# Eight instead of 55 extra pieces in the products of zeros at the head of a fused attention and feed-forward kernel

## The chip, the cores and the metric

The kernel runs on one core of a Trainium2 chip. The metric is the device time of one execution in microseconds, lower is better. Engines: TensorE (PE, with weight loads PEld and products), VectorE (DVE), ScalarE (ACT), GpSimd (POOL), SyncE (SP, which here issues DMAs only).

## The reference

Two parts, one after the other. The first is an attention in which keys and values are mixed block by block by a matrix P (8x8 for each batch and head) that five rounds of exponential and normalisation make from sort_net:

```python
# q, k, v: (4, 8, 768, 64); sort_net: (4, 8, 8, 8); block = 96
P = sort_net
for _ in range(5):
    P = np.exp(P - P.max(-1, keepdims=True))
    P = P / (P.sum(-1, keepdims=True) + 1e-09)
    P = P / (P.sum(-2, keepdims=True) + 1e-09)
k_sorted = einsum('bhij,bhjcd->bhicd', P, k_b)      # v_sorted likewise
scores = (q_b @ k_sb^T) / 8                         # inside a block of 96
attn = softmax(scores)
x = (attn @ v_sb) -> (3072, 512)
```

The second is a feed-forward over the 3072 rows: `h = x @ w_in` (512 to 2048), `g = h * cos(h)`, `out = g @ w_out` (2048 to 512).

## The kernel before

The rows of x are made in eight groups n = 0 to 7 of 384 rows (half a batch each), with four blocks u of 96 in a group. A table written out by hand, PLAN, sets the order in which every engine gets its work: a line such as `S 2 0 B` calls the function S with its arguments, and each engine works through its own instructions in that order. The calls that matter here:

- `v0`, `vb`, `vg`: products that mix the blocks of v (into `vS`); `vp`, `vp2` copy v into another order on POOL (`vperm`, L992), which some of these products read.
- `S` / `T`: scores; `M`, `X`: row maximum and difference on DVE; `E`: exponential on ACT into one of three buffers `p_buf`; `TP` / `TE` or `TD`: the transpose of p, by PE in the first groups and by a transposing DMA on SP's queue (L1396) in the later ones; `AV` (L1423): attention times values, whose weights are the transposed p; `N`: its normalisation on DVE; `XP` / `XE` or `XD` (L1445): the transpose into `xT`, by PE or by a transposing DMA.
- `U` (L1487): x times w_in; `C`: the sine on ACT; `G`: the product on DVE; `D` (L1532): g times w_out; `O`, `W`: out to memory.

Before the table runs, the head of the kernel issues the loads of q, k and v (POOL's queue, in that order, then w_in), and the five rounds on P run on ACT and DVE. Meanwhile PE multiplies zeros: `warm` is a 128x128 tile of zeros, and `keep_warm(times, t, cols)` (L1052) issues `times` products of `cols` columns into a tile that nothing reads. As long as `pieces` (L1050, set from MORE) lasts, a product is cut into up to four pieces of the same total of columns, each piece with a weight load and a product of its own. The head has, in this order: 15 (L1062, ahead of the first transposes of q, `q_twice`, L1135), 2 (L1157), and 6, 2 and 4 through `idle` (L1143). Later single calls in the first part of the plan (in `kp`, `v0`, `TP`, `AV`) come after `pieces` has run out.

With 55, all 15 opening products are cut in four (45 extra pieces), then the 2 (6 extra), then one of the first `idle` in four and one in two.

Of the kernel before, what the change touches and what calls it, by code (L numbers as in the profile page):

```python
# [13 lines left out]
ALU = mybir.AluOpType  # L14
AX = mybir.AxisListType

MORE = 55
PLAN = """\
vp 32
kp 0 B 1  # L20
# [811 lines left out]
def kernel(  # L832
# [16 lines left out]
    B, H, S, D = q.shape  # L849
# [129 lines left out]
    vv = kv[:, :128 * D].rearrange("p (c d) -> p d c", d=D)  # L979
    VQ = 16  # L980

    def v_permute(rows, lo=0, halves=True):

        for z in range(lo, D, VQ):
            dst = vperm[rows, :CD].rearrange("p (d c) -> p d c", d=D)[:, z:z + VQ]
            src = vv[rows, z:z + VQ, :blk]
            if halves:
                dst = dst.rearrange("p d (x t) -> p d x t", x=2)  # L990
                src = src.rearrange("p d (t x) -> p d x t", x=2)
            nc.gpsimd.tensor_copy(dst, src)  # L992
# [56 lines left out]

    pieces = [MORE]  # L1050

# [526 lines left out]
    def vp(lo):  # L1578
        v_permute(slice(0, 64), lo, False)

    def vp2(lo, hi):
        v_permute(slice(lo, hi))

    def z_vperm():
        nc.gpsimd.memset(vperm[:64, :D // 2 * blk], 0.0)

# [13 lines left out]
    def spv():  # L1600
# [4 lines left out]
        vb=vb, vbe=vbe, vg=vg, vge=vge, S=S, M=M, X=X, E=E, TD=TD, TP=TP, TE=TE, AV=AV, N=N,  # L1605
        XD=XD, XP=XP, XE=XE, QP=QP, QE=QE, QD=QD, U=U, C=C, G=G, U4=U4, C4=C4, G4=G4, D=D4,
        O=O, W=W, Lq=load_q, Lw=load_w_out, Lk=Lk, Lv=Lv, Lpk=Lpk, Lpv=Lpv, hk=hk, hp=hp_, hq=hq,
        vp=vp, vp2=vp2, z_vperm=z_vperm, p_pads=p_pads, pk2=pk2, bl2=bl2, sp2=sp2, spv=spv,
        ones=ones, z_turned=z_turned, zeros=zeros_between)
    words = {"A": (A,), "V": (V,), "B": (big, "big"), "c": (acc, "acc"), "-": (None,)}  # L1610
    for line in PLAN.split("\n"):
# [47 lines left out]
```

## Time and profile before

| | |
|---|---|
| median of 3 runs | 236.39 us (236.24 to 236.46) |
| profiled execution | 237.13 us, of which the span from first to last instruction is 235.3 us |
| PE busy, products | 96% of the span, 2270 recorded |
| PE weight loads | 62%, 2293 |
| DVE, ACT, POOL busy | 73%, 64%, 40% |
| granted clock of PE, mean | 0.998 |
| read from and written to memory | 27.27 MB and 6.29 MB |

The profile is one execution. A line such as `1.00 5.78 PE L1058 ...` gives start and duration in us, engine, line of the kernel, operation, what is written and read, shapes and count; in brackets is how long the engine stood idle before it and what ended that. Queues of DMAs have a line each with packets, MB and the time of these packets as a share of 16 DMA engines; "q8 instruction" is the queue on which instructions are fetched.

### The profile page before, as it was taken

The page shows a single profiled execution, that of the slowest core. Times are in us where ns is not written, and L with a number is a line of the kernel's source. Part 1 is how long each engine was busy: PE and PEld are TensorE (multiplying, and loading weights), DVE is VectorE, ACT ScalarE, POOL GpSimd, SP SyncE. Part 2 cuts the span into 40 slices and gives each one's busy share as a digit, 9 for nine tenths or more (in the row PEclk, how much of TensorE's full clock was granted, in tenths as well). Part 3 has the DMA queues.
Part 4 walks back from the last instruction along what each step waited for, and adds up shares of the span by engine and source line. Part 5 has one row for each costly group of instructions (what it writes and reads, how often), then busy time and mean ns, then how long its engine had stood idle before and what let it go on. Part 6 is the DMA issues. An engine that isn't in the chain of part 4 may idle for free.

```text
span 235.3 us, 5542 instructions
## 1 busy us (share of the span) xinstructions
PE 226.5 (96%) x2270; PEld 146.0 (62%) x2293; DVE 172.3 (73%) x287; ACT 151.3 (64%) x201; POOL 93.8 (40%) x117
## 2 busy tenths in 40 slices
PE   8889999999999999999999999999999999999994
PEld 8567799667656666645666556654565556456553
DVE  5657986787798786896678976899588868555510
ACT  3365976578969858884888746756567456636531
POOL 7669998795980094981709000720000000000000
PEclk9999999999999999999999999999999999999999
DMA  5999999796799779997999539995942570341012
GB/s 75 225 192 205 205 210 231 121 219 174 110 105 178 152 137 147 135 204 160 148 162 84 80 75 133 219 73 103 168 161 51 100 170 0 63 131 45 0 47 89
DMA packets 67257, 31.11 MB, mean 132 GB/s; under 512 B 55968, under 2 KB 62752, under 8 KB 66976
## 3 DMA queue, kind: packets, MB, share of 16 engines
q0 software_dynamic: 24048, 13.64, 44.0%
q1 hardware_dynamic: 42896, 16.92, 35.2%
q8 instruction: 18, 0.29, 0.5%
q10 hardware_dynamic: 288, 0.20, 0.3%
q14 instruction: 7, 0.06, 0.1%
HBM read 27.27 MB, written 6.29 MB: 143 GB/s over the span
## 4 chain that ended last, share of the span: by engine, by line
PE 82%; DMA 7%; ACT 3%; POOL 3%; DVE 2%; issue 2%; POOLq 0%
PE o L1532 32%; PE h L1487 29%; DMA kv<-in_v_dram 5%; PE h L1510 5%; PE av L1423 3%; PE sc L1319 3%; POOL vperm L992 2%; PE ks L1200 2%; PE xps L1457 2%; PE o L1623 2%; PE pps L1405 1%; DMA kv<-p_buf 1%; PE vs L1256 1%; PE vs L1291 1%; ACT c L1493 1%
## 5 line engine op out<-in xcount | busy, mean ns | idle before, releaser
L1532 PE MATMUL o<-w_out_t,gg 128*128 128x512 bf16 x348 | 84.7, 379 | 1.2 <-issue 0.2
L1487 PE MATMUL h<-xT,w_in_t 128*128 128x384 bf16 x448 | 78.2, 326 | 0.4 <-DVE gg L1499 0.2
L1499 DVE TENSOR_TENSOR gg<-c,h 128x768 bf16<-128x768 f32 x56 | 53.0, 949 | 22.4 <-ACT c L1493 22.3
L1493 ACT ACTIVATE c<-h,half_pi 128x768 f32<-128x768 f32 x56 | 50.5, 901 | 25.5 <-PE h L1487 23.3
L1487 PEld LDWEIGHTS <-w_in_t 128*128 128x128 bf16 x448 | 42.4, 98 | 27.5 <-issue 0.9
L1532 PEld LDWEIGHTS <-gg 128*128 128x128 bf16 x368 | 33.3, 98 | 33.0
L1360 DVE TENSOR_REDUCE mx<-sc 96x8 f32<-96x768 f32 (+1 forms) x41 | 31.5, 771 | 3.1 <-PE sc L1319 1.5
L1378 ACT ACTIVATE p_buf<-s 96x768 bf16<-96x768 f32 x32 | 26.3, 841 | 10.1 <-DVE s L1374 7.7
L992 POOL COPY vperm<-kv 64x1536 bf16<-64x1536 bf16 (+1 forms) x10 | 28.1, 2860 | 2.1 <-DMA kv<-in_v_dram 2.1
L1374 DVE TENSOR_TENSOR s<-sc,mx 96x384 f32<-96x384 f32 (+1 forms) x33 | 24.2, 734 | 1.6
L1435 DVE TENSOR_TENSOR xn<-av,r 96x512 bf16<-96x512 f32 x32 | 22.0, 687 | 1.1
L942 POOL DMA_DIRECT2D kv<-in_q_dram x24 | 16.0, 687 | 0.8 <-issue 0.5
L1069 ACT CAST kTs<-ks 128x512 bf16<-128x512 f32 (+1 forms) x18 | 11.0, 633 | 4.8 <-PE ks L1200 4.8
L942 POOL DMA_DIRECT2D q_mem<-in_q_dram x16 | 10.7, 695 | 3.4 <-DMA kv<-in_v_dram 3.1
L1058 PE MATMUL idle<-warm 128*128 128x128 bf16 (+2 forms) x83 | 9.5, 288 | 2.2 <-ACT q_turned L1141 1.2
L1433 DVE RECIPROCAL r<-av 96x8 f32<-96x8 f32 x32 | 6.3, 198 | 6.6 <-PE av L1423 6.6
L1071 DVE COPY kv<-o 128x512 f32<-128x512 f32 (+1 forms) x6 | 3.7, 624 | 10.0 <-PE o L1623 6.8
L1510 PE MATMUL h<-xT,w_in_t 128*128 128x192 bf16 x128 | 11.1, 246 | 0.0
L1319 PE MATMUL sc<-kTs,q_turned 128*128 128x96 bf16 x160 | 11.1, 206 | 0.0
L1058 PEld LDWEIGHTS <-warm 128*128 128x128 bf16 x101 | 8.9, 121 | 3.4 <-issue 1.3
L1319 PEld LDWEIGHTS <-q_turned 128*128 128x128 bf16 x160 | 9.1, 98 | 2.7 <-DVE s L1374 0.2
L1555 POOL CAST held<-q_turned 96x1 f32<-96x1 bf16 x2 | 0.4, 184 | 26.2 <-DMA q_turned<-q_mem 19.3
(119 smaller groups left out, 272.6 us busy)
## 6 DMA issues: line engine op xcount, KB each, us to landing
out_dram<-kv SPq DMA_DIRECT2D x12, 256.0 KB, 2.9
out_dram<-o_s SPq DMA_DIRECT2D x10, 256.0 KB, 3.0
w_in_t<-in_moe_w_in_dram POOLq DMA_DIRECT2D x4, 512.0 KB, 12.4
w_out_t<-in_moe_w_out_dram POOLq DMA_DIRECT2D x4, 512.0 KB, 11.6
kv<-in_k_dram POOLq DMA_DIRECT2D x2, 768.0 KB, 9.5
kv<-in_v_dram POOLq DMA_DIRECT2D x2, 768.0 KB, 13.3
pair<-in_k_dram POOLq DMA_DIRECT2D x2, 768.0 KB, 10.2
kv<-in_v_dram POOLq DMA_DIRECT2D x6, 256.0 KB, 5.7
```

What stands on the lines that cost most here:

```text
L942: nc.gpsimd.dma_start(out=q_heads[:, i, :, e], in_=src[:, ih * IC + i, :, e])
L992: nc.gpsimd.tensor_copy(dst, src)
L1319: nc.tensor.matmul(out, q_of(n, hp)[:, x:x + 128], keys_of(n, u, h2, hp), start=True, stop=True)
L1360: nc.vector.reduce_max(mx[:], s_view(n, u, hp), axis=AX.XY if n < 2 else AX.X)
L1374: nc.vector.tensor_tensor(s, sc, mx.to_broadcast(list(s.shape)), op=ALU.subtract)
L1378: nc.scalar.activation(p[:, :, :blk], s_t.pop((n, u)).rearrange("p e h c -> p (e h) c"), AF.Exp, scale=scale)
L1435: nc.vector.tensor_tensor(xn.rearrange("p h e d -> p e h d"), avv[:, :, :, :D], r.to_broadcast([blk, 2, H2, D]), op=ALU.mult)
L1487: nc.tensor.matmul(o[:, f2, x * w:(x + 1) * w], w_in_t[:, kk, f * 128:(f + 1) * 128], xT[n][:, kk, x * w:(x + 1) * w], start=(kk == 0), st ...
L1493: nc.scalar.activation(c[:], ps["h", n, fp][:, :, :TC], AF.Sin, bias=half_pi[:, 0:1])
L1499: nc.vector.tensor_tensor(gt[n, fp // 2][:, f:f + 2], ps.pop(("c", n, fp))[:], ps.pop(("h", n, fp))[:, :, :TC], op=ALU.mult)
L1510: nc.tensor.matmul(o[:, part, f2 * w:(f2 + 1) * w], w_in_t[:, kk, f * 128:(f + 1) * 128], xT[0][:, kk, h * w:(h + 1) * w], start=(kk == 0) ...
L1532: nc.tensor.matmul(out_ps[n, ts][:], gt[n, q][:, f % 4, ts * 128:(ts + 1) * 128], w_out_t[:, f, :], start=(f == 0), stop=(f == FC - 1))
```

## The change

`MORE` is 8 instead of 55. The first two opening products are cut in four and the third in three; all that follow are whole, of 512 columns. The columns of each call are the same, and 47 weight loads and 47 products are fewer. The code that builds the program also gets a function `vq` and an upper end for `v_permute`, which the plan does not call.

```diff
-MORE = 55
+MORE = 8
...
-    def v_permute(rows, lo=0, halves=True):
+    def v_permute(rows, lo=0, halves=True, hi=D):
...
-        for z in range(lo, D, VQ):
+        for z in range(lo, hi, VQ):
...
+    def vq(lo, hi, z):
+        v_permute(slice(lo, hi), z * VQ, True, (z + 1) * VQ)
```

On PE, at the end of the cut part of the opening products; before, the last pieces ahead of the transposes of q (`qps` from `q_mem`):

```order
L1058 MATMUL idle<-warm 128x128
L1058 LDWEIGHTS warm
L1058 MATMUL idle<-warm 128x128
L1135 LDWEIGHTS q_mem
L1135 MATMUL qps<-ident,q_mem 64x4x24
```

and now, where the cut products pass into whole ones:

```order
L1058 MATMUL idle<-warm 128x128
L1058 LDWEIGHTS warm
L1058 MATMUL idle<-warm 128x170
L1058 LDWEIGHTS warm
L1058 MATMUL idle<-warm 128x171
L1058 LDWEIGHTS warm
L1058 MATMUL idle<-warm 128x171
L1058 LDWEIGHTS warm
L1058 MATMUL idle<-warm 128x512
L1058 LDWEIGHTS warm
```

The first transpose of q is PE's row 121 of 4588 before, and row 47 of 4494 now.

On PE, in the first `idle` (six products between two lots of transposes of q), before:

```order
L1058 MATMUL idle<-warm 128x128
L1058 LDWEIGHTS warm
L1058 MATMUL idle<-warm 128x256
L1058 LDWEIGHTS warm
L1058 MATMUL idle<-warm 128x256
L1058 LDWEIGHTS warm
L1058 MATMUL idle<-warm 128x512
```

and now, up to the transposes behind them, all of them whole:

```order
L1058 MATMUL idle<-warm 128x512
L1058 LDWEIGHTS warm
L1058 MATMUL idle<-warm 128x512
L1135 LDWEIGHTS q_mem
L1135 MATMUL qps<-ident,q_mem 64x4x24
```

From here on PE's rows are the same, each 94 earlier in its stream of instructions: the first product of `bl` (L1180) is row 297 before and row 203 now. The rows of DVE, ACT, POOL and SP are as many as before (250, 149, 65 and 54) and in the same order.

More of the change, by code (lines that the diff above doesn't have):

```diff
@@ L1607 @@
         O=O, W=W, Lq=load_q, Lw=load_w_out, Lk=Lk, Lv=Lv, Lpk=Lpk, Lpv=Lpv, hk=hk, hp=hp_, hq=hq,
-        vp=vp, vp2=vp2, z_vperm=z_vperm, p_pads=p_pads, pk2=pk2, bl2=bl2, sp2=sp2, spv=spv,
+        vp=vp, vp2=vp2, vq=vq, z_vperm=z_vperm, p_pads=p_pads, pk2=pk2, bl2=bl2, sp2=sp2, spv=spv,
         ones=ones, z_turned=z_turned, zeros=zeros_between)
```

## Prediction

> **What bounds the kernel.** I read the page first, then the chain of waits, the start of the timeline, the DMA queues in narrow stretches, and the stretches around the transposing DMAs.
>
> ```profile
> PE 226.5 (96%) x2270; PEld 146.0 (62%) x2293; DVE 172.3 (73%) x287; ACT 151.3 (64%) x201; POOL 93.8 (40%) x117
> q8 instruction: 18, 0.29, 0.5%
> PE 82%; DMA 7%; ACT 3%; POOL 3%; DVE 2%; issue 2%; POOLq 0%
> ...
> 2.72 12.68 DMA kv<-in_v_dram
> 15.46 5.57 POOL vperm L992 x2
> 21.81 0.94 PE vs L1256 x16
> ```
>
> TensorE (PE) is busy nearly throughout and carries 82% of the chain, so a delay on PE after about 21 us is a delay of the end. Before that, the chain is not PE: it is the load of v (to 15.40), the two POOL copies that it releases, and only then PE. The second line matters later: PE's instructions come from memory in 18 blocks of 16 KB. For 4563 recorded PE instructions that is a block for every 253.
>
> ```profile
> 1.00 5.78 PE L1058 MATMUL idle<-warm 128*128 128x128 bf16 x60 [1.00 <-DVE half_pi L1041]
> 6.94 0.87 PE L1135 MATMUL qps<-ident,q_mem 96*64 96x96 bf16 x32 [0.16 <-DMA q_mem<-in_q_dram]
> 7.74 0.63 PE L1058 MATMUL idle<-warm 128*128 128x128 bf16 x8
> 12.72 1.03 PE L1058 MATMUL idle<-warm 128*128 128x512 bf16 x4 [0.49 <-ACT q_turned L1141]
> 21.07 0.20 PE L1256 MATMUL vs<-bdv,vperm 64*128 64x64 bf16 x1 [0.34 <-POOL vperm L992]
> 21.54 0.95 DVE L1360 TENSOR_REDUCE mx<-sc 96x8 f32<-96x768 f32 x1 [0.48 <-PE sc L1332]
> ```
>
> The opening zeros end at 6.78 and PE then waits for q anyway. At 21.07 PE waits for the POOL copy, and VectorE (DVE) stands idle 0.48 us behind it.
>
> **Part 1, the zeros themselves.** Columns are the same. Eight pieces step at (0.63 - 0.22) / 7 = 0.059 us, taking 0.22 us for one; four whole products step at (1.03 - 0.38) / 3 = 0.217. So a call in four pieces costs 0.235 and a whole one 0.217: some ten calls become whole, 0.02 us each. The opening pieces take 5.78 / 60 = 0.096 us, a slower array, where no row shows a whole product. Its bounds: the same per column (end near 6.7), or twice the later 0.217 to the end, 12 x 0.434 + 8 x 0.107 + 3 x 0.145 = 6.5 us, an end at 7.5, 0.6 us after q is there. The 60 pieces are nearest, and cover q's wait. Cost taken: 0, with +0.3 as the upper end, since after q the normalisation on DVE and ScalarE (ACT) has its own chain.
>
> **Part 2, where the blocks of instructions are fetched.** 47 products fewer are 94 PE instructions fewer, all before 13 us; every later block boundary falls 94 instructions, 47 products, later in the work. The first fetch shows why that is not nothing. These are the queues from 11.8 to 12.9 us, and the count from 13.6 to 14.9:
>
> ```profile
> DMA packets 17, 0.21 MB, mean 194 GB/s; under 512 B 0, under 2 KB 0, under 8 KB 0
> q0 software_dynamic: 16, 0.20, 85.2%
> q8 instruction: 1, 0.02, 5.5%
> ...
> DMA packets 251, 0.27 MB, mean 206 GB/s; under 512 B 1, under 2 KB 250, under 8 KB 250
> ```
>
> The load of v moves in packets of 0.20 MB / 16 = 12 KB, each 0.852 x 16 x 1.1 / 16 = 0.94 us of an engine. The fetch takes 0.055 x 16 x 1.1 = 0.97 us of one of those engines. After 13.6 a single packet above 8 KB is left among the small ones of w_in: one engine is about a packet behind, and v lands with it. 47 products after 11.9 is about 15 us, when v is through. So v lands 0.9 to 1.1 us earlier, the POOL copies end near 20.0, and the wait at 21.07 goes. What is late next is DVE, whose previous operation ends at 21.54 - 0.48 = 21.06: gain 0.48, not 1.0. From there DVE, ACT and PE run as one chain into the dense products of the feed-forward part. Bounds: 0 (the fetch comes early and still sits ahead of v's end) to -0.5. I take **-0.48**.
>
> **Part 3, the fetches that move onto transposing DMAs.** Two stretches between fetches, and four stretches each of about 47 products after a fetch (columns: PE busy, PEld, DVE, ACT, POOL, clock, DMA share, GB/s):
>
> ```profile
> 126.71:141.04 14.33, 14.21 (x127) 7.80 (x127) 12.48 (x20) 9.34 (x14) 2.32 (x4) 1.00 0.62 76
> 141.04:156.61 15.57, 15.52 (x121) 9.45 (x121) 12.68 (x19) 11.38 (x12) 5.53 (x9) 1.00 1.10 155
> ...
> 102.04:106.80 4.76, 4.76 (x54) 2.21 (x54) 4.47 (x7) 4.28 (x6) 2.92 (x2) 1.00 0.93 196
> 126.71:131.90 5.19, 5.12 (x49) 2.79 (x48) 4.54 (x7) 4.87 (x7) 2.32 (x4) 1.00 0.89 58
> 156.61:161.30 4.69, 4.53 (x49) 2.25 (x48) 4.52 (x7) 1.37 (x3) 0.00 (x0) 1.00 0.99 103
> 173.70:180.00 6.30, 6.25 (x49) 3.24 (x49) 5.86 (x8) 5.39 (x6) 0.00 (x0) 1.00 0.01 3
> ```
>
> The blocks follow PE's count. So the fetches now at 102.0, 126.7, 156.6 and 173.7 go to the places that PE reaches today at 106.8, 131.9, 161.3 and 180.0. What a fetch does to a transposing DMA is seen around 156.6 (the queues from 156.6 to 158.2, then GB/s in three stretches) and on SP's queue:
>
> ```profile
> q8 instruction: 1, 0.02, 5.8%
> ...
> 156.50:157.40 0.90, 0.90 (x6) 0.36 (x4) 0.90 (x2) 0.00 (x0) 0.00 (x0) 1.00 3.13 161
> 157.40:158.60 1.20, 1.04 (x20) 0.65 (x20) 1.17 (x2) 0.00 (x0) 0.00 (x0) 1.00 0.04 4
> 158.60:160.30 1.70, 1.70 (x16) 0.80 (x15) 1.60 (x3) 1.31 (x2) 0.00 (x0) 1.00 0.81 153
> ...
> 104.41 1.27 SPq L1396 DMA_TRANSPOSE kv<-p_buf  x1
> 131.74 1.22 SPq L1396 DMA_TRANSPOSE kv<-p_buf  x1
> 133.07 2.55 SPq L1396 DMA_TRANSPOSE pT<-p_buf  x2
> 139.84 3.62 SPq L1396 DMA_TRANSPOSE vperm<-p_buf  x2
> 155.35 3.83 SPq L1396 DMA_TRANSPOSE vperm<-p_buf  x2
> 159.28 3.81 SPq L1445 DMA_TRANSPOSE xT<-xn  x3
> 179.21 2.55 SPq L1396 DMA_TRANSPOSE vperm<-p_buf  x2
> ```
>
> 161 GB/s fall to 4 for 1.2 us, 0.8 us after the fetch began, and two pairs of issues take 3.83 and 3.62 us (the second beside the fetch at 141.04, the bound of two rows above) where others take 2.55: 1.1 to 1.3 us for each transpose that a fetch meets. Whether that reaches PE is read from the weight loads that wait:
>
> ```profile
> 107.52 0.32 PEld L1423 LDWEIGHTS <-kv 96*128 96x128 bf16 x8 [0.46 <-DMA kv<-p_buf]
> 134.58 0.38 PEld L1423 LDWEIGHTS <-kv 96*128 96x128 bf16 x8 [0.26 <-DMA kv<-p_buf]
> 159.91 0.32 PEld L1423 LDWEIGHTS <-vperm 96*128 96x128 bf16 x8 [0.41 <-DMA vperm<-p_buf]
> 164.29 0.78 PEld L1487 LDWEIGHTS <-w_in_t 128*128 128x128 bf16 x6 [0.56 <-issue]
> 182.04 0.44 PEld L1423 LDWEIGHTS <-vperm 96*128 96x128 bf16 x8 [0.20 <-DMA vperm<-p_buf]
> ```
>
> - At 131.9: the transpose issued at 131.74 is what the product at 134.58 already waits for, without slack. A stop from 132.7 to 133.9 costs it 0 to 1.3; I take **+0.8**, as the issue ends at 132.96 and part of the stop is before its data.
> - At 161.3: a stop from 162.1 to 163.3 falls on the third xT transpose (issued from about 161.8), behind which stand the U products at 164.29. 0 to 1.3, taken as +0.9. The old meeting at 156.6 goes; its product waited 0.41 as a weight load, about half of that in PE: -0.2. Net **+0.7**.
> - At 180.0: the product at 182.04 waits for a transpose issued at 179.21. 0 or 1.2; a stop from 180.8 may find it mostly done. Taken as 0, the 1.2 kept as a rival.
> - At 106.8: the product at 107.52 waits for the transpose of 104.41, whose data must be nearly through by then. 0 to 1.1, taken as 0.
> - The other fetches move to stages without a transposing DMA, or in front of one that is wanted microseconds later: 0, and cover is lost only if those stages tighten.
>
> The Trainium skill (Runtime: NRT & Kernel Launch, Instruction fetch mechanics) says that an engine's instruction store is refilled in 16 KiB blocks of 256 instructions while it executes, and that crossing a block costs one DMA tail-bump, mostly hidden. The trace agrees with the block's size (16 KB, 253 instructions) and shows no wait of PE that it puts down to missing instructions; but the page counts only PE's own wait, and by it the sum would be 0, the second rival below.
>
> **Sum.** 0 - 0.48 + 0.8 + 0.7 = +1.0 us on a span of 235.3. The profiled execution took 237.13 us in all, 0.74 above the median of the runs; I put the difference on the median: 236.39 + 1.0 = **237.4**. A measurement of this kernel can tell about 0.2%, 0.47 us, from no change.
>
> **Rivals.**
> 1. The fetches miss the transposes that have no slack. The trace shows when a block moves, not when it is asked for, so the 47 products hold to a microsecond or so, and fetches at 130.5 and 160 would be done before the data of those two transposes move. Then only the gains stand: -0.48 - 0.2, **235.7**, faster. It decides at the place of two fetches, against transposes of 1.2 us.
> 2. Fetches are hidden, v's last packet is late for another reason, and a stop of the transposes is not the fetch's: no change, **236.4**. For it: PE shows no wait on instructions. Against: the stop at 157.4 and the long pair at 139.84 both coincide with a fetch.
> 3. The fetch at 180.0, or that at 106.8, meets its transpose too: 237.4 + 1.2 = **238.6**.
> 4. The coarser zeros delay the rise of the array's pace, up to +0.3: inside the ranges, no case of its own.
>
> **Chances.** Forecast 0.40 (0.34 slower, 0.06 within 0.2%; its own range 236.8 to 238.0, one of the two terms at 0 or both at 1.3). Rival 1: 0.16 (0.15 faster). Rival 2: 0.19 (0.02 faster, 0.17 same). Rival 3: 0.25, slower. Together faster 0.17, same 0.24, slower 0.59. The range goes from rival 1 to just above rival 3: 235.6 to 238.8.
>
> **What would show it.** In the profile after: the opening zeros end by 6.9; the load of v in the chain near 11.6 us instead of 12.68, POOL's copy at 14.4, no wait of PE on vperm near 21; fetch packets about 47 products later; SP issues that take 1.2 us more near 132 and 162, with the product after the first waiting about 1 us for kv<-p_buf, and the issues at 139.84 and 155.35 back to 2.55. The prediction is wrong if the issues near 132 and 162 keep 1.2 us each, or if PE's waits there don't grow.

## The result, and the profile after

The changed kernel took **240.08 us** (median of 4 runs, 239.79 to 240.30) beside 236.43 for the kernel before (4 runs): +3.65 us, ratio 1.0138, 95% interval 1.0114 to 1.0163. The forecast was 237.4, range 235.6 to 238.8. The direction was right, the size was not. The profiled execution took 240.30 with a span of 238.5, against 237.13 and 235.3 before, so the two traces differ by 3.2 us. When the changed kernel was run again (last experiment), runs of 241 to 243 turned up too; one of them was traced and is shown there. Single runs far above the others of their kernel (251 in e2, 240.84 in e3, 244 to 246 in e5) are in a slow state and are left out of the ratios.

The page after (engines, the queue of instructions, the chain) and the waits of PE (line waited for: us in total, times, longest):

```profile
PE 228.4 (96%) x2246; PEld 142.7 (60%) x2246; DVE 172.3 (72%) x287; ACT 151.3 (63%) x201; POOL 93.8 (39%) x117
...
q8 instruction: 17, 0.28, 0.5%
...
PE 72%; DVE 11%; DMA 7%; ACT 5%; issue 2%; POOL 1%; POOLq 0%; ACTq 0%; DVEq 0%
```

```profile
PE sc L1346 <- DMA kTs<-kTs: 1.8, 1, 1.8
...
PE av L1423 <- DMA vperm<-p_buf: 0.8, 1, 0.8
PE h L1487 <- DMA xT<-xn: 0.7, 1, 0.7
PE av L1423 <- DMA kv<-p_buf: 0.4, 1, 0.4
```

One block of instructions fewer, and three waits for DMAs that the kernel before did not have: 3.3 us together. The first is for `kTs<-kTs`, two copies of keys inside SBUF (`kswap`, L1244 and L1245, 384 KB each), which the prediction never named.

The weight loads are the same in both programs from q's turning on, so their starts can be subtracted one by one. The difference (after minus before) changes at these places; the value is the one that holds behind each place, which the first loads there can miss by up to 0.25:

| at (before, us) | difference behind it | what happened there |
|---|---|---|
| 21.07 | -0.50 | v is there earlier |
| 80.3 | -0.27 | AV's weight load waits for a transposed tile, a fetch at 77.2 beside it: +0.23 |
| 106.87 | +1.75 | wait for the key copy: +2.02 |
| 134.6 | +1.75 | the place where +0.8 was forecast: nothing |
| 159.9 | +1.70 | the old meeting gone: -0.05 |
| 164.22 | +2.30 | wait for xT: +0.60 |
| 182.04 | +3.28 | wait for vperm: +0.98 |
| end | +3.20 | -0.08 in small steps |

The timeline at those places (start, busy us, engine, line, and the idle time before):

```profile
1.00 5.80 PE L1058 MATMUL idle<-warm 128*128 128x128 bf16 x23 [1.00 <-DVE half_pi L1041]
6.91 0.87 PE L1135 MATMUL qps<-ident,q_mem 96*64 96x96 bf16 x32
...
14.25 5.52 POOL L992 COPY vperm<-kv 64x1536 bf16<-64x1536 bf16 x2 [0.72 <-DMA kv<-in_v_dram]
...
108.57 0.33 PE L1346 MATMUL sc<-kTs,q_turned 64*128 64x96 bf16 x7 [1.77 <-DMA kTs<-kTs]
...
166.63 1.46 PE L1487 MATMUL h<-xT,w_in_t 128*128 128x384 bf16 x8 [0.69 <-DMA xT<-xn]
...
185.45 0.43 PE L1423 MATMUL av<-pair,vperm 96*128 96x65 bf16 x8 [0.80 <-DMA vperm<-p_buf]
```

In the kernel before, PE takes the same keys without a wait, and the two transposes of p beside them take 2.57 us to issue:

```profile
106.87 0.33 PE L1346 MATMUL sc<-kTs,q_turned 64*128 64x96 bf16 x8
```

```profile
105.78 2.57 SPq L1396 DMA_TRANSPOSE pT<-p_buf  x2
```

What SP's queue and the DMAs did after the change, around the places of loss (SP's issues; then, for the largest loss, stretches with PE, PEld, DVE, ACT, POOL, clock, DMA share, GB/s; then the queues from 106.2 to 107.2):

```profile
105.56 3.79 SPq L1396 DMA_TRANSPOSE pT<-p_buf  x2
...
159.74 5.65 SPq L1445 DMA_TRANSPOSE xT<-xn  x3
...
181.51 3.25 SPq L1396 DMA_TRANSPOSE vperm<-p_buf  x2
```

```profile
104.50:106.20 1.70, 1.70 (x9) 0.69 (x7) 1.67 (x4) 1.25 (x3) 0.00 (x0) 1.00 0.87 209
106.20:107.20 1.00, 0.60 (x19) 0.32 (x18) 0.49 (x1) 1.00 (x2) 0.00 (x0) 1.00 2.66 86
107.20:108.30 1.10, 0.00 (x0) 0.00 (x0) 0.00 (x0) 0.76 (x1) 0.00 (x0) 1.00 0.06 7
108.30:109.30 1.00, 0.35 (x8) 0.21 (x8) 0.36 (x1) 0.00 (x0) 0.00 (x0) 1.00 1.17 257
```

```profile
q1 hardware_dynamic: 272, 0.07, 259.7%
q8 instruction: 1, 0.02, 6.0%
```

A fetch starts at 106.596, 2 ns after the key copy's last 6 KB packet ended at 106.594, and runs to 107.556. Of the transposes of p, fifteen packets of 256 bytes begun at 106.28 to 106.59, and five more begun by 106.86, stand still (7 GB/s) and end together at 108.31 to 108.36. The fifteen took 1.7 to 2.06 us each; waiting packets that overlap are why the "share" is 259.7%. PE gets the keys at 108.57. Two nanoseconds (and again two in e11, 106.437 and 106.439) suggest that the copy's last packet and the fetch were on one engine, with the copy's completion behind the fetch; the trace does not name the engine.

From 107.54 to 108.31 the trace shows some 30 packets of 256 bytes one behind the other, a new one about every 0.03 us, and then the others end at once. e3 shows the same behind its fetch (102.20 to 102.97). This fits one engine that the fetch held, working off its share while the rest wait for it; as engines are not named, it is argued and not shown.

### The profile page after: what moved, and what is told of

Its sections match the earlier page's. It is cut to its first block, busy times and chain, and to the rows that moved or that the text cites. A ratio compares the mean times of both kernels' runs of the same rounds, so it can differ in the third digit from the quotient of the medians.

```text
span 238.5 us, 5471 instructions
## 1 busy us (share of the span) xinstructions
PE 228.4 (96%) x2246; PEld 142.7 (60%) x2246; DVE 172.3 (72%) x287; ACT 151.3 (63%) x201; POOL 93.8 (39%) x117
## 4 chain that ended last, share of the span: by engine, by line
PE 72%; DVE 11%; DMA 7%; ACT 5%; issue 2%; POOL 1%; POOLq 0%; ACTq 0%; DVEq 0%
PE h L1487 27%; PE o L1532 23%; PE h L1510 4%; PE av L1423 3%; DVE gg L1499 2%; PE vs L1256 2%; DMA kv<-p_buf 2%; PE ks L1200 2%; PE sc L1319 2%; DVE mx L1360 2%; DVE s L1374 2%; ACT c L1493 2%; DMA vperm<-p_buf 2%; DMA pT<-p_buf 2%; PE o L1626 1%
## 5 line engine op out<-in xcount | busy, mean ns | idle before, releaser
L1532 PE MATMUL o<-w_out_t,gg 128*128 128x512 bf16 x368 | 87.4, 379 | 0.0
L1487 PEld LDWEIGHTS <-w_in_t 128*128 128x128 bf16 x448 | 42.4, 98 | 28.1 <-issue 1.5
L1058 PE MATMUL idle<-warm 128*128 128x512 bf16 (+3 forms) x37 | 9.5, 419 | 2.2 <-ACT q_turned L1141 1.2
L942 POOL DMA_DIRECT2D q_mem<-in_q_dram x16 | 10.7, 690 | 2.1 <-DMA kv<-in_v_dram 1.7
L1510 PEld LDWEIGHTS <-w_in_t 128*128 128x128 bf16 x128 | 10.4, 98 | 0.0
```

The lines of the kernel that those rows point to most:

```text
L942: nc.gpsimd.dma_start(out=q_heads[:, i, :, e], in_=src[:, ih * IC + i, :, e])
L1487: nc.tensor.matmul(o[:, f2, x * w:(x + 1) * w], w_in_t[:, kk, f * 128:(f + 1) * 128], xT[n][:, kk, x * w:(x + 1) * w], start=(kk == 0), st ...
L1510: nc.tensor.matmul(o[:, part, f2 * w:(f2 + 1) * w], w_in_t[:, kk, f * 128:(f + 1) * 128], xT[0][:, kk, h * w:(h + 1) * w], start=(kk == 0) ...
L1532: nc.tensor.matmul(out_ps[n, ts][:], gt[n, q][:, f % 4, ts * 128:(ts + 1) * 128], w_out_t[:, f, :], start=(f == 0), stop=(f == FC - 1))
```

## The experiments

The question is whether the places of the fetches make the time, or the coarser zeros, or the number of instructions as such. All ratios are to the kernel before, run beside it on the same chip (236.8 there).

**e1: coarse opening zeros, same number of instructions.**

```
-    pieces = [MORE]
+    pieces, most = [MORE], [3]
...
-            n = 1 + min(3, pieces[0])
+            n = 1 + min(most[0], pieces[0])
...
     keep_warm(15, big.tile([128, 512], FP32, name="idle", tag="big"))
+    pieces[0], most[0] = 47, 4
```

> The opening zeros stay as in the changed kernel (8 more pieces); the 47 pieces that the change took away are cut from the 14 later calls of zeros instead, all still before 13.7 us, same columns. So the zeros of the start are coarse, while the PE instructions ahead of everything that follows number as many as in the kernel before. Theory of places (a fetch of instructions is harmless or dear by where it falls in the work): the fetches fall back to where they lay before (102, 126.7, 156.6, 173.7), the waits of PE for kTs (1.8), xT (0.7) and vperm (0.8) go, 236.4 (235.9 to 236.9). Theory of zeros (the coarse opening itself costs, by the array's pace or by what starts when): 240.1.

Measured 236.92, ratio 1.0007 (0.9992 to 1.0021). The fetches lie at 101.8, 126.8, 156.5 and 174.0, within half a microsecond of before's, and the three waits are gone. This decides between the opening zeros and places: the opening is as coarse as in the changed kernel and costs nothing. (The later zeros are cut finer here than in either kernel; e9, which has all zeros of the changed kernel, closes that gap.) The gain on v is gone too, the first fetch being ahead of v's end again (at 13.6). From e1's chain, and its waits of PE:

```profile
2.74 12.84 DMA kv<-in_v_dram
15.63 5.54 POOL vperm L992 x2
```

```profile
PE vs L1257 <- POOL vperm L992: 0.4, 1, 0.4
```

**e2: fine opening zeros, fetches as in the changed kernel.** As e1, with

```
-MORE = 8
+MORE = 55
...
+    pieces[0], most[0] = 10 + 81, 7
```

> The opening zeros in 55 pieces more as before the change; the later 14 calls are cut further, 81 products of zeros more, 162 PE instructions. 162 more instead of 94 fewer is the same place within a block of 256, so from the second fetch on all fall where they fall in the changed kernel, with one more ahead of them. Same columns of zeros. Theory of places: the losses of the changed kernel come back, waits of PE for kTs 1.8, xT 0.7, vperm 0.8; 240.1 (239.4 to 240.9; the upper end if the extra early fetch holds up the load of v). Theory of zeros: 236.4. Theory of numbers (fewer or more instructions matter as such): below 236.4 or not above it by over 0.5.

Measured 242.66 (239.43 to 251.15), ratio 1.0208 (1.0163 to 1.0253): slower with the finest zeros of all, which only the theory of places allows, but 1.8 over the top of its range. The waits of PE, the stretches behind the wait for keys (the granted clock stands before the DMA share), and one row of PE's timeline:

```profile
PE av L1424 <- DMA kv<-p_buf: 1.7, 2, 1.4
PE sc L1347 <- DMA kTs<-kTs: 1.4, 1, 1.4
PE av L1424 <- DMA vperm<-p_buf: 1.2, 1, 1.2
```

```profile
108.00:109.00 1.00, 0.33 (x7) 0.18 (x6) 0.18 (x1) 0.20 (x1) 0.00 (x0) 1.00 1.09 239
109.00:110.00 1.00, 0.73 (x10) 0.54 (x12) 0.90 (x2) 0.00 (x0) 0.00 (x0) 0.86 0.90 163
110.00:111.00 1.00, 1.00 (x3) 0.38 (x3) 0.97 (x3) 0.00 (x0) 0.00 (x0) 0.50 0.73 139
```

```profile
139.46 0.43 PE L1424 MATMUL av<-pair,kv 96*128 96x65 bf16 x8 [1.35 <-DMA kv<-p_buf]
```

Two things were not expected. PE's clock fell to 0.50, products of 512 columns stepped at 0.43 us instead of 0.22, and the work from 109.3 to 113.5 came 1.7 us later relative to the changed kernel's. And the product that the prediction charged with +0.8, unharmed in the changed kernel, waits 1.35 here: the fetch began at 137.28, when the transpose's data were moving, and from 138.2 to 139.1 the DMAs moved 52 GB/s. The wait for xT that was expected did not come; that fetch fell at 170.8, about 4 us later in the work than in the changed kernel's trace. The lower end, 239.43, is one run, of which there is no trace.

**e3 and e4: move only the later fetches.** The changed kernel with 94 weight loads of one column that no product uses, one behind each dense product from a given place in the plan on.

```
 AV 2 0
+pad 94
...
+    def lone():
+        if spare[0]:
+            spare[0] -= 1
+            nc.tensor.ldweights(warm[:, spare[0] % 2:spare[0] % 2 + 1])
...
                         xT[n][:, kk, x * w:(x + 1) * w], start=(kk == 0), stop=(kk == KC - 1))
+                    lone()
...
                 w_out_t[:, f, :], start=(f == 0), stop=(f == FC - 1))
+            lone()
...
+    def pad(n):
+        spare[0] = n
```

> The changed kernel, with 94 weight loads of one column that no product uses, one behind each dense product between about 80 and 100 us. They restore the count of instructions behind them, so the fetches after 100 us fall as in the kernel before, the ones up to 80 us as in the changed kernel. Each load costs from 0 (under a dense product of 0.16 us whose own load takes 0.10) to 0.027 (the step of small loads), 0 to 2.5 in all. Theory of places: the losses of 1.9 at 106.6, 0.65 at 164 and 1.1 at 182 go and the 0.25 at 160 comes back: 240.1 - 3.65 + 0.25 = 236.7 plus the loads' cost. Theory that these waits come from what starts earlier or later at the head: 240.1 plus the loads' cost, with the wait for kTs still there.

In e4 the line `pad 94` stands behind `AV 3 1` instead.

> The same 94 loads, but between about 109 and 133 us, behind the place of the key copy. Theory of places: the wait for kTs near 106.6 stays at 1.8, the losses at 164 and 182 go, the 0.25 at 160 comes back: 240.1 - 1.75 + 0.25 = 238.6 plus the loads' cost, and e3_lone_before is faster than this by 1.9. Other theories: no difference between this and e3_lone_before.

Measured: e3 238.02, ratio 1.0063 (1.0036 to 1.0089); e4 238.66, 1.0081 (1.0053 to 1.0110). The loads cost nothing that shows: behind them, at 102 us, e3 runs 0.16 ahead of the changed kernel. e4 came out as expected in its median: the wait for keys stays and the waits at 164 and 182 are gone. (Its traced run, 239.71, lies above the median, with a wait for keys of 2.3.) e3 missed by 1.3. The waits at 164 and 182 are gone there too, but one for keys is left, of 1.2. Its waits of PE, SP's issue of the second key copy, and two stretches say why:

```profile
PE sc L1353 <- DMA kTs<-kTs: 1.2, 1, 1.2
```

```profile
101.24 1.69 SPq L1252 DMA_DIRECT2D kTs<-kTs  x1
```

```profile
100.50:101.50 1.00, 0.95 (x13) 0.57 (x15) 0.81 (x1) 0.64 (x1) 1.00 (x2) 1.00 2.89 221
101.50:102.50 1.00, 1.00 (x5) 0.57 (x9) 0.70 (x1) 0.98 (x2) 1.00 (x1) 1.00 0.31 5
```

The fetch began at 101.26, not at 102.05, and met the tail of q's transposes, which stand ahead of the key copy: 221 GB/s fall to 5 for a microsecond, and the copy is late by that; so e3 is faster than e4 by 0.6 only, where 1.9 was expected. So the same copy was held up from the other side, and "the fetches fall as before" has to hold to half a microsecond.

**e5: put the pieces behind v's load, in the small products.** As e1, but the line `pieces[0], most[0] = 47, 7` stands ahead of the loop over the plan.

> The changed kernel, with the 47 pieces put back in the seven calls of zeros between 14.2 and 21 us, which stand ahead of products on keys and v: the first fetch stays behind the load of v, all later ones fall as in the kernel before. Same columns of zeros. Theory of places: the gain on v stays (0.5 to 0.6), all of the losses of the changed kernel go: 236.2 where before is 236.8 (235.9 to 236.6); a fetch that falls on the transposes of q near 101 would add 1.2. Theory of zeros: 240.

Measured 237.57, ratio 1.0023 (1.0006 to 1.0040), with four of twelve runs at 244 to 246. A miss. The profiled run is one of the four (245.6), so it cannot say what the other eight do; around 19 us it shows a thing that no other trace here has (PE's timeline, then two stretches):

```profile
18.79 0.35 PE L1332 MATMUL sc<-kTs,q_turned 64*128 64x64 bf16 x8
19.85 0.25 PE L1332 MATMUL sc<-kTs,q_turned 64*128 64x64 bf16 x6 [0.70 <-issue]
```

```profile
18.00:20.00 2.00, 1.29 (x29) 1.11 (x25) 0.52 (x1) 0.59 (x1) 2.00 (x2) 1.00 1.22 201
20.00:22.00 2.00, 2.00 (x30) 1.68 (x24) 1.82 (x2) 0.41 (x1) 2.00 (x4) 0.52 1.24 206
```

In the middle of a row of equal products PE stands for 0.70 with no releaser. The first fetch began at 17.62, some 50 instructions before that point, and ended at 18.59. That this is PE waiting for its instructions fits, since eight 64-column pieces now use up 16 instructions in 0.42 us, but no run took the fetch away, so it is argued and not shown. Behind it the clock is 0.5 for some 20 us. There is no trace of the runs at 237.3, so why they miss the forecast stays open.

**e6: spare only the place at 182.** As e4, with `pad 94` behind `XE 5 3 A`.

> The changed kernel, with the 94 weight loads that no product uses put between about 166 and 181 us, behind the places at 106.6 and 164 and ahead of that at 182. In the traces of e3_lone_before and e4_lone_after such loads cost nothing. Theory of places: the fetch of 182.7 moves to about 177, where no transposing DMA is under way; PE's wait for vperm (0.8, 1.1 with its weight loads) goes alone, the waits for kTs (1.8) and xT (0.7) stay: 239.0 (238.4 to 239.5). If the wait at 185 comes from the delays ahead of it and not from the fetch: 240.1.

Measured 241.04 (five runs of 241.00 to 241.12 and one of 238.72), ratio 1.0163 (1.0130 to 1.0196). Its waits of PE, and a stretch behind the wait for keys:

```profile
PE sc L1353 <- DMA kTs<-kTs: 1.6, 1, 1.6
...
PE h L1494 <- DMA xT<-xn: 0.8, 1, 0.8
```

```profile
109.40:113.00 3.60, 3.55 (x16) 1.41 (x14) 2.17 (x4) 0.00 (x0) 1.67 (x4) 0.59 0.62 150
```

The waits are what places say: keys and xT stay, vperm is gone, with the fetch at 179.4. The time is not, because the clock fell here too, which cost 1.7 us by the starts of the weight loads. The trace ends 0.7 behind the changed kernel's; without the fall it would end 1.0 ahead, against 1.1 expected.

**e7 and e8: other numbers of pieces.** `MORE = 31` and `MORE = 75`, nothing else.

> 31 pieces more, about half way between 55 and 8: 48 PE instructions fewer than before. Theory of zeros, or of anything that grows with the number taken away: 236.8 + 3.65 x 24 / 47 = 238.7. Theory of places: the fetches fall near 103.8 (inside the key copy's packets, 0 to 0.9), 128.9, 144.2 and 159.0 (on the first transpose of xT, 0 to 1.2), 177.0 (nothing there); v gains 0 to 0.6: 236.8 (236.2 to 238.2), with no wait for vperm near 182.

> 75 pieces more, 40 PE instructions more than before, finer zeros than before. Theory of zeros: 236.8 or below. Theory of places: the fetches fall near 99.8 (on the transposes of q that stand ahead of the key copy, 1.2 as in e3_lone_before), 124.4, 138.3 (on xT, not awaited soon), 155.2, 170.7, 186.5: 237.8 (236.8 to 238.6), with a wait for kTs near 107.

Measured: e7 237.72, ratio 1.0049 (1.0027 to 1.0070); e8 237.82, 1.0045 (1.0031 to 1.0059). More pieces than before and fewer are both slower, so the time does not follow their number. e7 lies between the two theories' numbers, inside the range of places; its trace has the wait for keys that the fetch at 104.3 was given (0.8), none for vperm at 182. e8 has the forecast time by another place than forecast: no wait for keys, but 1.0 for vperm at 205, where a fetch at 204.4 meets transposes. The waits of PE, of e7 and then of e8:

```profile
PE sc L1346 <- DMA kTs<-kTs: 0.8, 1, 0.8
```

```profile
PE av L1423 <- DMA vperm<-p_buf: 1.0, 1, 1.0
```

**e9, e10 and e11: a version without losses, and the changed kernel again.** e9 is e3 with two loads behind each dense product, started ahead of `D 0 0 0` (43 us):

```
+pad 94
 D 0 0 0
...
-        if spare[0]:
+        for _ in range(min(2, spare[0])):
```

> The changed kernel, with 94 weight loads that no product uses, two behind each dense product of 0.22 us between 43 and 56 us, where PE takes few instructions for its time. The first fetches stay as in the changed kernel (behind the load of v), those from about 56 us on fall as in the kernel before. Theory of places: gain on v 0.5 to 0.6, no losses: 236.2 where before is 236.8 (235.9 to 236.6), without the wait for instructions that e5_behind_v had near 19; 237.4 if the fetch near 102 comes early enough for the transposes of q (as at 101.26 in e3_lone_before). If this too is not below 236.6, the gain on v is not one at the end.

e10 has `pad 134` there and `pad 32` behind `XE 6 3 A`.

> As e9_lone_early with 40 loads more behind the dense products to 68 us, and 32 more at 193 to 196. In e8_more75, whose fetches lie 40 instructions earlier than before's, PE lost nothing up to 204, then 1.0 to a fetch at 204.4 on the transposes that a product of 205.5 waits for; the 32 loads move that one to about 202, ahead of the transposes' data. Theory of places: 237.8 - 1.0 - 0.4 (v) = 236.4 (236.0 to 237.0), without a wait over 0.4 for a transposed tile.

> The changed kernel itself once more, beside the others on one chip. In e2_same_phase and e6_lone_late the granted clock fell to 0.5 for some 3.5 us behind the wait for kTs, in the changed kernel's profile it did not. If that fall comes with the length of the wait alone, it shows here too in some of the runs, 242; if it belongs to those two kernels, all runs lie at 239.8 to 240.5.

Measured: e9 **236.31**, ratio 0.9985 (0.9972 to 0.9998): the fastest kernel of the study, by a little under half a microsecond, as forecast from the gain on v, though the interval ends just short of 1. Its weight loads at 60 and at 78 us start within 0.01 us of the changed kernel's, so the 94 added ones cost nothing. POOL's copy starts at 14.03, and PE's longest wait for a DMA is 0.3:

```profile
14.03 5.49 POOL L993 COPY vperm<-kv 64x1536 bf16<-64x1536 bf16 x2 [0.49 <-DMA kv<-in_v_dram]
```

```profile
PE av L1430 <- DMA kv<-p_buf: 0.3, 1, 0.3
```

e10: 237.17, 1.0028 (1.0008 to 1.0048), 0.2 above its range: the fetch meant for 202 began at 202.4, took 1.38 us and still held the transposes behind it (wait for vperm 0.6). Its fetch near the key copy, at 98.2 where the first of q's transposes ends, costs no wait for keys.

e11: 241.28 (239.83 to 242.97), 1.0194 (1.0154 to 1.0235). The changed kernel too has runs with the lower clock, so the expectation that these belong to two kernels only is out. One stretch in the control, and the same in the changed kernel's first profile:

```profile
109.40:113.00 3.60, 3.41 (x14) 1.27 (x12) 2.10 (x4) 0.00 (x0) 1.60 (x4) 0.54 0.59 148
```

```profile
109.40:113.00 3.60, 3.60 (x25) 1.71 (x24) 2.25 (x4) 0.00 (x0) 1.31 (x3) 1.00 0.63 153
```

14 products instead of 25 in 3.6 us, and 1.7 us lost by the starts of the weight loads. So the fall belongs to some runs, and not to the kernels e2 and e6. The mean granted clock of every run says where it can occur: runs at 0.991 to 0.993, as in the traces with the fall, turn up in e2, e3, e4, e6, e7 and e11, all of which wait for the keys, and in no run of before, e1, e8, e9 or e10, which do not (0.997 or more). A few long runs have no such clock (240.63 and 241.02 of e11, 242.83 of e2, 241.11 of e6: 0.998 to 1.0); they have no trace, and why they are long stays open.

In the control's trace the wait for xT is missing: the fetch that was at 163.85 in the changed kernel's first trace is at 169.54, with the work only 1.9 later. The same kernel can have the same fetch 4 us elsewhere in the work.

**All fetches beside the key copy.** One fetch of each kernel falls near the key copy, and PE's wait for the keys goes with its place:

| kernel | fetch starts | beside | wait for kTs |
|---|---|---|---|
| e8, e10 | 98.1, 98.2 | first of q's two transposes, in e10 its end | none |
| e3 (work 0.4 earlier) | 101.26 | tail of q's second transpose | 1.2 |
| e9 (work 0.5 earlier) | 101.33 | first packets of the copy | none |
| e1, before | 101.8, 102.0 | first packets of the copy | none |
| e5 (work 8.6 later) | 110.01 | first packets of the copy | none |
| e7 | 104.3 | the copy's second half (70 of 128 packets through) | 0.8 |
| e2, e4 | 105.9, 106.4 | the copy's last packets (92 and 102 through) | 1.4, 2.3 |
| e6, e11, after | 106.3, 106.4, 106.6 | the copy's end (127, all, all through), transposes of p | 1.6, 1.7, 1.8 |

In the last row the copy's last packet ends at 106.4 to 106.6, only 0.3 to 0.4 later than in the kernel before (106.17), but PE gets the keys 1.98 to 2.00 us behind it. In e2, e3, e4 and e7, where the last packets come late (106.7 to 108.7), PE has the keys 0.64 to 1.09 behind them. So most of the wait in the changed kernel is for what follows the last packet.

And one goes with v: where the first fetch starts at 10.7 to 13.6 (before, e1, e2, e8), POOL's copy starts at 15.32 to 15.63; where it starts at 14.1 or later (the nine other traces), at 14.03 to 14.63. From 25 us on the weight loads of these nine stand 0.48 to 0.50 ahead of before's (e5 apart, behind its stop), and those of e1, e2 and e8 between 0.17 ahead and 0.14 behind.

## Why the prediction was right or wrong

- **The zeros cost 0**: right. The 23 opening products end at 6.80 and q's products start at 6.91; e1 shows no cost of the coarse opening in the time.
- **v, -0.48**: right in cause and size. -0.50, by thirteen traces on one side or the other of v's end.
- **Where the fetches go**: right, to 0.8 us at the four places. Less the delay that has gathered by then, they lie at 106.9, 131.8, 162.1 and 180.4, for 106.8, 131.9, 161.3 and 180.0 forecast. (The first lies at 17.3, for about 15.)
- **+0.8 at 131.9**: wrong, nothing came. The fetch (133.59 to 134.63) began 0.1 after the transpose's issue and was over before its data moved; the trace has no other packet beside it. So this place was missed, as in the first rival, though the fetch lay where it was forecast. e2, with the fetch 2 us later in the work, shows the charge was possible: 1.35.
- **+0.7 at 161.3**: right, +0.60 (and -0.05 where -0.2 was counted for the old meeting). The issue of the three xT transposes grew from 3.81 to 5.65. Of the two long pairs from which the price was read, only one was wholly the fetch's: the pair at 155.35 went from 3.83 back to 2.55, that at 139.84 (3.62) still takes 3.13 with no fetch beside it.
- **0 at 180.0**: wrong, +0.98. This was the third rival's price of 1.2.
- **0 at 106.8**: wrong, and the step that failed most: +2.02, more than its upper bound of 1.1. The step looked for transposing DMAs only, at one product (107.52). The key copy ends there as well; in the kernel before its last packet ends at 106.17, 0.7 us before PE takes the keys. As it caused no wait before, no row of waits named it. It should have been looked for among the transfers whose landing lies shortly before their use.
- **"The other fetches: 0"**: wrong by 0.23 at 80.3 (a fetch at 77.2 on p's transposes).
- **The sum**: -0.50 + 0.23 + 2.02 - 0.05 + 0.60 + 0.98 - 0.08 = 3.2 in the traces; the medians differ by 3.65, since the traced run of before lay 0.7 above its median and that of after 0.2 above its own. Of four possible meetings the forecast priced two in part and two at 0, and three came. Of the third rival, "180.0 or 106.8", both came.
- **The direction**: right, but by luck. The terms that the forecast priced came to -0.50 + 0 + 0.60 - 0.05 = +0.05 together; the whole loss came from places that it had put at 0.
- **Second rival, fetches hidden**: out. The Trainium skill (Runtime: NRT & Kernel Launch, Instruction fetch mechanics) calls the crossing of a block mostly hidden. For PE's own supply that holds in every trace but perhaps one (e5, 0.70). The transfers beside it are another matter: e1 against the changed kernel, and e9 with the same zeros, show over 3 us by place alone.

## What to carry to other kernels

Taking away or adding instructions on a long engine program moves the later fetches of instructions, so an edit at the head can cost or gain microseconds far behind it: look for the fetch packets in the trace before blaming the edited lines, and restore the count in a place that is idle as a control. The transfers to fear for are the ones that are spread over many DMA engines and that land shortly before their use (the losses here were 0.2 to 2.0 us), plain copies as well as transposes, even if no wait is recorded for them. Weight loads that no product uses, behind dense products, move the fetches without a cost of their own (e3, e9), but a gain tuned so hangs on the place of a fetch to half a microsecond (e3 against e9).

## What the runs showed of the hardware that was not expected

- A fetch of 16 KB, one packet of 0.9 to 1.7 us, stopped the transposing DMAs under way at 106.6 (after) and at 101.3 (e3): packets of 256 bytes took up to 2.06 us, and some 210 GB/s fell to 7 and 5.
- PE's granted clock fell to 0.50 for 3.4 us after waits of 1.4 to 1.7 and 0.35 us close together (e2, e6, e11), at 1.7 us each, and did not after 1.8 and 0.4 (after) or 2.3 and 0.35 (e4). So the length of the wait does not decide it. The Trainium skill (TensorE: Matmul & The Clock Gate, HAM oscillation — how this bites in real kernels) tells of waits for DMAs of over 3.4 us that throttle the array again; the waits here were shorter and did it in some runs. The Trainium skill (TensorE: Matmul & The Clock Gate, What's actually happening) tells of an activity window that runs freely; a fall in some runs and not in others would fit that, but no run here tests it.
- The same head of the program had its first fetch at 15.1 in one trace (e3) and at 17.3 to 17.6 in others (after, e4, e9), and one kernel in two executions (after, e11) had a later fetch 4 us apart in the work. So a fetch's place in one profile holds to a few microseconds where PE waits and works by turns, or behind such waits.
